# A new order, engine choice and buffer choice for the 822 tasks of a sparse attention and maxout kernel

## The chip, the cores and the metric

The kernel runs on one NeuronCore of a Trainium2 chip. Its five engines run their own instruction queues in order: TensorE (PE in the profile) for matmuls and transposes, VectorE (DVE), ScalarE (ACT), GpSimd (POOL) and SyncE (SP), which issues DMAs. Data moves between HBM and the on-chip memory SBUF by DMA; PE writes its results to eight banks of PSUM, which DVE and ACT read. The metric is device time in microseconds (us) of one execution, the median of several runs.

## The reference

Four batches, eight heads, 768 positions of 64 values. Each position attends to its neighbours closer than 16 and to 24 block summaries (the maximum of k, the mean of v over blocks of 32). A two-branch maxout layer follows, in which the two hidden products are compared element by element.

```python
k_sum = k.reshape(B, H, nb, block, D).max(axis=3)
v_sum = v.reshape(B, H, nb, block, D).mean(axis=3)
scores_l = np.where(mask_l, scale * q @ k.T, -1e9)
scores_s = scale * einsum('bhsd,bhnd->bhsn', q, k_sum) + log(block)
a = softmax(concatenate([scores_l, scores_s], axis=-1))
x = heads_side_by_side(a @ concatenate([v, v_sum], axis=2))   # 3072 x 512
out = np.maximum(x @ w1, x @ w2) @ w_out                       # 512 -> 1024 -> 512
```

Inputs and output are float32; the matmuls run in bf16.

## The kernel before, in words

The kernel writes the work down as a list of tasks (`Plan.op`): each has a label, the engines that could do it, the buffers it reads and writes, and a function that issues its instructions. `Plan.run` then sends the tasks out in an order given by hand (`CFG["order"]`, numbers of tasks), each on the engine that a letter names (`CFG["engines"]`: T for PE, D for DVE, A for ACT, P for POOL, S for SP) and into the buffer of a ring that a character names (`CFG["slots"]`). Each engine therefore runs its tasks in the order in which they stand in the list, and waits for what it reads, and for the last readers of a buffer that it writes again. Nothing else sets the order: there is no planner at run time.

A label such as `x 021` has the batch (0), the group of 256 positions (2) and the first of two pairs of heads (1 stands for its pair); `wd 10` has the half of the hidden units (1) and of the input rows (0). What the labels mean, in the order of the data:

- `load k03`, `load q03`, `load v03` (L334, L343): one pair of heads of one batch is loaded from HBM, 384 KB, by a DMA from SP into a ring of 13 buffers `land`. A load waits until the former content of its buffer has been read. Loads of k, and most of q, read runs of 1536 bytes (two to a partition), loads of v and of six q (w in the label) runs of 256.
- `cast` (L254 on POOL, L256 elsewhere): to bf16. POOL does it in two or three instructions.
- `turn k`, `turn q` (L463): transposes on PE into PSUM, followed by `place` (L256), the copy into SBUF. For six pairs of heads of batches 2 and 3, k and q, a transposing DMA from SP (`dturn`, L467) does this.
- `max k` (L487), `wrap`, `tails`, `sums k` (L256): the block maxima of k and the copies that put local keys and summaries side by side in `kx`.
- `odd v`, `sums`, `esums`, `all sums` (L387, L424, L254, L256): v in the second alignment, and the block sums of v, made on PE with `amean` and copied into `vx`.
- `hides` (L518, batch 0) or `mask` (L549): the positions that do not count. `scores` (L529), `exp` (L541, on ACT), `values` (L569), `inv` and `x` (L587, L590, on DVE): the attention. x goes into `xt` in transposed form, for batch 0 by PE (`turn x`, L605, and a copy `xt`), for the others by a transposing DMA (`dxt`, L596).
- `load w`, `load wo` (L620, L651), `wd` (L630, the difference of the two weights), `w1b`, `turn w1`, `w1t`, `wo`: the weights, once. `w1o` (L662) is w1 times w_out, so that out = x @ w1o + relu(x @ (w2 - w1)) @ w_out.
- `hidden` (L678), `relu` (L690 on ACT, L692 on DVE), `outx` and `outg0`, `outg1` (L715), `copy out` (L256), `store` (L729, and L731 where an output block wraps around the end of the batch): the layer after attention, in 12 groups of 256 positions, each with four hidden tasks of 8 matmuls (in batch 0 in two halves) and two outputs of 12 matmuls. The second half of the very last group (`320`) is cut into 256, 128 and 128 columns.
- `filler` (L750): 30 matmuls on zeros, whose result nobody reads.

The order of the tasks in `Plan.op` calls is fixed by the code; the three strings of CFG only say when, where and into which buffer.

Of the kernel before, what the change touches and what calls it, by code (L numbers as in the profile page):

```python
# [24 lines left out]
PPPDPDPPPDDPDPPPTTTTTTTTTTTTTTTTTTTTTTTTTTTTTTSSSPDDDTDDDSSSPADATDDPSSSADAATAPPSSSADDATAAASSPDTASSPATASSPDTDSSDDTASPSD  # L25
SPSAPTPTDDADDDDTPTDDAAADATATDDPPPDPTDTADPAADTTATTDDTDTTATTDDTATTATTDDTDTTATTDDTATTATTDDTATTATTDDTDSSSPSSSPSSSDSSSDDDAD
DPTDDAPDADAPATPTDDAAPDATATDDDDDADTPTDDDDPDPTATADAAAATADTTDDSTADTTDDSTADTTDDSTADTTDDSTADTTDDSTADTTDDSSSSASSSASSSPSSSDDD
PDDPPTDAPDDDPPDATPTDDDADDDTPTADDDPDPSASDDPPAASDSADAPATADTTDDSTADTTDDSTADTTDDSTADTTDDSTADTTDDSTADTTDDSSSSPSSSASSSPSSSDP
ADDAAPTDPPDAPPPADSPSADPPDDSDSDDAAPPSDSADADDASPSDDAAPTADTTDDSTADTTDDSTADTTDDSTADTTDDSTADTTDDSTADTTDDSTTATTATTATTATTATTA
TTATTDTTTDATTTDSTTDTTATTATTDTTTDSTTTDATTATTATTDTTATTTAATTTAATATDTATATTTAATTTASTATDTATATTTDSTTTAATATATDTATTTASTTTASTATD  # L30
TDTDTTTDATTTDSTDTATATDTTTDATTTDSTATATATATTTAATTTDSTATDTDTDTTTAATTTDSTDTDTDTDTTTAATTTDSTATATATDTTTASTTTAATTTAATTTDA
""".split())
CFG["order"] = list(map(int, """
# [778 lines left out]
```

## Time and profile before

| | |
|---|---|
| runs | 166.24, 166.53 and 202.32 us; median 166.53 |
| profiled execution | 168.04 us, of which 166.1 are the span from first to last instruction |
| busy in the span | PE 153.8, DVE 108.7, ACT 97.0, POOL 66.3 us |
| DMA | 36.48 MB, 25.18 MB read from HBM and 6.29 MB written to it |
| granted TensorE clock | 1.0 throughout |

The profile's page has, after the busy times, the span in 40 slices (each digit the busy share in tenths), the DMA queues, the chain of work that ended last, and groups of instructions by line, engine and shape with their busy time, the mean duration in ns, and the idle time of the engine just before them with what ended it. A timeline row has the start in us, the time in us, engine and line, output and inputs, and in brackets the idle time before it and its releaser. PE's busy time includes the fillers.

### The profile page before, as it was taken

What the parts mean: (1) busy time and instruction counts of PE and PEld (TensorE: products, weight loads), DVE (VectorE), ACT (ScalarE), POOL (GpSimd) and SP (SyncE); (2) the same over time, 40 slices, a digit from 0 to 9 for tenths busy, and PEclk for the clock granted to TensorE, in tenths of its full rate; (3) what the DMA queues carried; (4) which work ended last, traced back from release to release, by engine and by line L of the source; (5) the groups of instructions that cost most, each with busy time, mean ns of one, the idle gap of its engine ahead of it and who ended that gap; (6) DMA issues with size and microseconds to landing.
All of it is one profiled execution on the core that took longest, in us unless ns stands there. A gap on an engine that the chain in (4) does not pass through costs nothing.

```text
span 166.1 us, 4394 instructions
## 1 busy us (share of the span) xinstructions
PE 153.8 (93%) x1760; PEld 100.1 (60%) x1782; DVE 108.7 (65%) x210; ACT 97.0 (58%) x140; POOL 66.3 (40%) x136
## 2 busy tenths in 40 slices
PE   4696769999999999999999999999997999999995
PEld 1244456998655554577578555676545657756763
DVE  3188698739847699799598575759865777161310
ACT  3158999756897579648965596544666721010511
POOL 5876547952458076323699230010919000000000
PEclk9999999999999999999999999999999999999999
DMA  5999999999999999399899998799998515930354
GB/s 158 286 301 295 234 318 390 385 381 382 307 255 220 310 361 182 88 203 175 151 231 190 258 276 133 151 216 229 210 168 210 171 46 156 180 123 4 113 206 129
DMA packets 67988, 36.48 MB, mean 220 GB/s; under 512 B 54912, under 2 KB 61952, under 8 KB 67968
## 3 DMA queue, kind: packets, MB, share of 16 engines
q1 hardware_dynamic: 65648, 33.04, 81.6%
q10 hardware_dynamic: 2320, 3.16, 6.7%
q8 instruction: 14, 0.23, 0.6%
q14 instruction: 6, 0.05, 0.1%
HBM read 25.18 MB, written 6.29 MB: 189 GB/s over the span
## 4 chain that ended last, share of the span: by engine, by line
PE 69%; DMA 10%; DVE 5%; SPq 5%; ACT 4%; issue 2%; POOL 2%; POOLq 0%; DVEq 0%; ACTq 0%
PE banks L715 31%; PE banks L678 20%; DMA land<-in_k_dram 7%; SPq L334 5%; PE banks L662 4%; PE banks L569 4%; PE banks L463 3%; DMA kt<-kqb 3%; PE banks L529 3%; POOL vx L254 2%; DVE xs L590 1%; DVE vx L256 1%; ACT kqb L256 1%; PE banks L639 1%; PE banks L750 1%
## 5 line engine op out<-in xcount | busy, mean ns | idle before, releaser
L678 PE MATMUL banks<-xt,wd 128*128 128x256 bf16 x384 | 45.4, 273 | 0.9 <-DMA xt<-xs 0.9
L715 PE MATMUL banks<-wo,g 128*128 128x512 bf16 (+2 forms) x198 | 45.1, 362 | 0.9 <-issue 0.6
L678 PEld LDWEIGHTS <-wd 128*128 128x128 bf16 x384 | 37.0, 98 | 7.4 <-issue 1.1
L715 PEld LDWEIGHTS <-g 128*128 128x128 bf16 x208 | 19.1, 98 | 18.8
L541 ACT ACTIVATE pb<-banks 128x1024 bf16<-128x1024 f32 x24 | 23.6, 1021 | 7.8 <-PE banks L529 7.6
L690 ACT ACTIVATE g<-banks 128x512 bf16<-128x512 f32 x28 | 16.1, 598 | 17.3 <-PE banks L678 17.1
L715 PE MATMUL banks<-w1o,xt 128*128 128x512 bf16 (+2 forms) x96 | 23.8, 362 | 0.9 <-issue 0.3
L254 POOL CAST kqb<-land 128x256 bf16<-128x256 f32 (+1 forms) x35 | 16.3, 501 | 17.8 <-DMA land<-in_k_dram 7.7
L692 DVE TENSOR_SCALAR g<-banks 128x512 bf16<-128x512 f32 x20 | 13.4, 685 | 14.0 <-PE banks L678 13.3
L254 POOL COPY vx<-sums 32x396 bf16<-32x396 bf16 x26 | 15.7, 629 | 6.9 <-DVE sums L256 6.3
L256 ACT COPY o<-banks 128x512 f32<-128x512 f32 (+2 forms) x13 | 7.0, 544 | 18.0 <-PE banks L715 10.8
L590 DVE TENSOR_TENSOR xs<-banks,inv 128x512 bf16<-128x512 f32 x24 | 16.4, 690 | 0.6
L487 DVE TENSOR_REDUCE ks<-kx 128x24 bf16<-128x768 bf16 x16 | 14.9, 939 | 2.0 <-ACT kx L256 1.8
L715 PEld LDWEIGHTS <-xt 128*128 128x128 bf16 x104 | 9.6, 98 | 8.9 <-issue 0.4
L549 DVE TENSOR_TENSOR pb<-pb,mask 128x1024 bf16<-128x1024 bf16 x18 | 13.0, 750 | 2.2 <-ACT pb L541 2.1
L256 DVE COPY o<-banks 128x512 f32<-128x512 f32 (+1 forms) x13 | 8.3, 652 | 8.7 <-PE banks L715 8.7
L463 PE MATMUL banks<-ident,kqb 128*128 128x128 f32 x60 | 10.1, 279 | 2.7 <-DVE kqb L256 1.3
L569 PEld LDWEIGHTS <-pb 128*64 128x64 bf16 x384 | 7.7, 110 | 6.4 <-issue 4.0
L750 PE MATMUL banks<-zeros,identity 128*128 128x512 bf16 x27 | 9.4, 466 | 2.3 <-DVE identity L237 2.2
L463 PEld LDWEIGHTS banks<-ident,kqb 128*128 128x128 f32 x60 | 7.1, 140 | 6.2 <-ACT kqb L256 1.8
L569 PE MATMUL banks<-vx,pb 128*64 128x65 bf16 x384 | 9.6, 196 | 1.4 <-DVE vx L256 1.0
L256 ACT CAST kqb<-land 128x768 bf16<-128x768 f32 x10 | 9.5, 953 | 2.3 <-DMA land<-in_k_dram 2.1
(78 smaller groups left out, 179.2 us busy)
## 6 DMA issues: line engine op xcount, KB each, us to landing
land<-in_k_dram SPq DMA_DIRECT2D x16, 384.0 KB, 5.9
land<-in_q_dram SPq DMA_DIRECT2D x16, 384.0 KB, 6.3
land<-in_v_dram SPq DMA_DIRECT2D x16, 384.0 KB, 6.3
land<-in_moe_w_dram SPq DMA_DIRECT2D x8, 512.0 KB, 9.4
out_dram<-o ACTq DMA_DIRECT2D x10, 256.0 KB, 2.9
out_dram<-o SPq DMA_DIRECT2D x9, 256.0 KB, 3.3
land<-in_moe_w_out_dram SPq DMA_DIRECT2D x4, 512.0 KB, 10.1
out_dram<-o SPq DMA_DIRECT2D x3, 224.0 KB, 3.0
```

Source lines behind the costliest of these rows:

```text
L254: nc.gpsimd.tensor_copy(out=o[:, n * z:n * z + n], in_=i[:, n * z:n * z + n])
L256: {"D": nc.vector.tensor_copy, "A": nc.scalar.copy, "P": nc.gpsimd.tensor_copy}[e](out=o, in_=i)
L463: nc.tensor.transpose(out=bank(ps)[:, 128 * j:128 * j + 128], in_=src.ap[:].bitcast(F32)[:, 128 * j:128 * j + 128], identity=ident32[:])
L487: op("D", lambda e: nc.vector.tensor_reduce(out=ks.ap[:, 0:nb], in_=free(kt(), 128, [256, NM], [192, 2], [32, 2], [1, 32]), axis=AX.X, op= ...
L541: op("A", lambda e: nc.scalar.activation(out=spread(pb.ap[:, 0, 0:1], [1, 1024]), in_=spread(bank_tile[:, ps.ap, 0:1], [1, 1024]), func=AC ...
L549: on(e).tensor_tensor(out=o.rearrange("p n (u c) -> p n u c", u=2), in0=o.rearrange("p n (u c) -> p n u c", u=2), in1=in1, op=ALU.mult)
L569: nc.tensor.matmul(out=av(n)[64 * par:64 * par + 64, u, a, :], lhsT=pb.ap[r, at, 64 * par:64 * par + 64], rhs=rhs, start=start, stop=stop)
L590: op("D", lambda e: nc.vector.tensor_tensor(out=x.ap[:].rearrange("p n u a d -> p n (u a) d"), in0=spread(bank_tile[:, ps.ap, 0:1], [512, ...
L678: nc.tensor.matmul(out=bank(ps)[:, 256 * s:256 * s + 256], lhsT=wd[n // 2][:, c, 256 * (n % 2) + 128 * s:256 * (n % 2) + 128 * s + 128], r ...
L690: nc.scalar.activation(out=o, in_=bank(ps), func=ACT.Relu)
L692: nc.vector.tensor_scalar_max(out=o, in0=bank(ps), scalar1=0.0)
L715: nc.tensor.matmul(out=bank(ps, c1 - c0), lhsT=a, rhs=w, start=(i == j == 0), stop=(i == 2 and j == 3))
```

## The change

All three strings are replaced; the functions that make the tasks stay as they are, so both kernels have the same 822 tasks with the same dependencies. The order, the engine letters and the buffer characters were searched anew against a replay in which shared ports and queues are granted strictly in order of time. The diff, cut to its first and last lines:

```diff
 CFG["engines"] = "".join("""
-PPPDPDPPPDDPDPPPTTTTTTTTTTTTTTTTTTTTTTTTTTTTTTSSSPDDDTDDDSSSPADATDDPSSSADAATAPPSSSADDATAAASSPDTASSPATASSPDTDSSDDTASPSD
...
+PDPPDPDDPDPPDDPPTTTTTTTTTTTTTTTTTTTTTTTTTTTTTTSSSDDDDTADADSSSPDAPTDAPSSSAAAPTADASSSADDPTDDDSSPATASSPATASSDATDSSDATDSDSD
...
 CFG["order"] = list(map(int, """
-26 33 36 24 23 39 43 38 19 17 25 13 8 1 10 79 46 57 152 2 14 153 156 9 11 6 12 132 133 136 122 123 126 137 158 3 138
...
-814 815 816 37 29 35 20 28 45
+46 44 8 10 41 21 24 38 20 79 36 122 43 25 26 32 42 123 40 17 6 5 9 11 3 13 152 2 14 12 7 16 198 126 127 59 60 64 28 65
...
+802 803 793 804 30 805 806
 """.split()))
 CFG["slots"] = "".join("""
-21307350100567735176041164504713:20254416874209;71<0001211340787130912213221010031111222322013302361011622101070220060
...
+32131016101270510013030211110705722362618:40019;01<0061215541436000821000202020332111303323112210200000104042246161121
...
 """.split())
```

Read out, with the numbers turned into labels:

| | before | after |
|---|---|---|
| tasks on PE, DVE, ACT, POOL, SP | 291, 207, 153, 69, 102 | 291, 223, 150, 51, 107 |
| cast of k or q on DVE, ACT, POOL | 9, 10, 13 | 12, 11, 9 |
| cast of v on DVE, ACT, POOL | 4, 5, 7 | 7, 5, 4 |
| all sums on DVE, ACT, POOL | 11, 8, 13 | 15, 10, 7 |
| wd on DVE, POOL | 1, 3 | 2, 2 |
| wo (cast) on DVE, ACT, POOL | 1, 1, 2 | 3, 1, 0 |
| relu on ACT, DVE | 28, 20 | 25, 23 |
| stores from ACT, SP | 14, 12 | 9, 17 |

SP's queue begins, before: k03, k00, k01, q00, v01, q01, k02, v02, q02, q03, v00, v03, then w100, w200, w201, w101, w110, w210, k11, k13, w211, w111. After: k00, k03, v01, k01, v02, q00, q01, v00, k02, q03, q02, v03, then w100, w200, w101, w201, w111, w210, w110, w211, k12, wo1, k10, k13, k11.

PE's queue begins, before, with 11 fillers and turn k03, k01, k00, q00; further fillers stand up to just ahead of the first hidden task (hidden 0200, with turn x 021 ahead of it), and six at the very end. After, 12 fillers, turn k00, and 17 more fillers between hides, sums and turns, all ahead of the first scores; the first hidden task is 0210, with turn w1 00, turn x 021 and turn x 022 ahead of it; one filler stands at the end.

The last attention of batch 3, before: scores 300, 301, 302, later 320, 322, 321. After: scores 321, 320, 322, later 302, 301, 300. PE's queue ends, before: outputs 321, then 320 in its three pieces. After: hidden 310, the pieces of 320 between outputs 300 and 301, then outputs 311, 310, 311 (its last part) and 321.

More of the change, by code (lines that the diff above doesn't have):

```diff
@@ L29 @@
-ADDAAPTDPPDAPPPADSPSADPPDDSDSDDAAPPSDSADADDASPSDDAAPTADTTDDSTADTTDDSTADTTDDSTADTTDDSTADTTDDSTADTTDDSTTATTATTATTATTATTA
-TTATTDTTTDATTTDSTTDTTATTATTDTTTDSTTTDATTATTATTDTTATTTAATTTAATATDTATATTTAATTTASTATDTATATTTDSTTTAATATATDTATTTASTTTASTATD
-TDTDTTTDATTTDSTDTATATDTTTDATTTDSTATATATATTTAATTTDSTATDTDTDTTTAATTTDSTDTDTDTDTTTAATTTDSTATATATDTTTASTTTAATTTAATTTDA
+PDPPDPDDPDPPDDPPTTTTTTTTTTTTTTTTTTTTTTTTTTTTTTSSSDDDDTADASSSPDAPTDAPSSSAAAPTADASSSADDPTDDDSSPATASSPATASSDATDSSDATDSDSD
+SDSAATPTDDAAADPTDTDDADDADTPTDDAADDPTDTDDPPPDTTATTDDTDTTATTDDTDTTATTDDTATTATTDDTDTTATTDDTATTATTDDTDSSSDSSSASSSDSSSDADDP
@@ new lines @@
+ADTDADDDDDDDDTDTADPPADDTATDDPAPAPTDTADDADDATDTDDAAPATADTTDDSTADTTDDSTADTTDDSTADTTDDSTADTTDDSTADTTDDSSSSPSSSPSSSDSSSADD
+AADAATAAAPPDPPDATATADPDADPTATDDPAPDDSASDDDDDASPSDDAPATADTTDDSTADTTDDSTADTTDDSTADTTDDSTADTTDDSTADTTDDSSSSDSSSPSSSASSSDD
+DPDAPDTAAAPPDADAPSASDDAPADSDSDDPADASASADDADDSPSDDDDATADTTDDSTADTTDDSTADTTDDSTADTTDDSTADTTDDSTADTTDDSTTATTDTTATTATTATTA
+TTATTATTTASTTTASTTATTDTTDTTDTTTDSTTTASTTATTATTDTTATTTDSTTTASTATDTDTDTTTAATTTDSTDTATDTDTTTASTTTDSTDTATDTATTTASTTTAATATD
+TATDTTTDSTTTASTDTATATATTTAATTTDATDTDTDTATTTDSTTTDSTDTDTATATTTDATTTASTATATATDTTTAATTTDSTDTATDTATTTAATTTDSTTTDATTTDA
@@ L68 @@
+432033426227224010096;;37794:5<2032350140212325171220124251000221334340121420400423040025232115020813:9468<02371231203
+2102300041032212204412143000222212204036121000342218;10:47<32651100151212042013330025213164402562420212133444016361142
+0223263042323746551271406270115616361037541202326627020077407421302100510021021162733030550676234531054645102655451076
 """.split())
```

6 lines of the change are left out of this document (removed), and 52 rows, old and new, of the table turn.

## The prediction

> **What bounds the kernel now.** I read the page's first two parts, then the busy time in three stretches cut at the first matmul of the hidden layer (29.27 us) and at the last matmul of an output (163.1 us), then who made PE wait in the middle stretch.
>
> ```profile
> span 166.1 us, 4394 instructions
> PE 153.8 (93%) x1760; PEld 100.1 (60%) x1782; DVE 108.7 (65%) x210; ACT 97.0 (58%) x140; POOL 66.3 (40%) x136
> DMA  5999999999999999399899998799998515930354
> ```
>
> ```profile
> core 0: us, PE busy (x) PEld busy (x) DVE busy (x) ACT busy (x) POOL busy (x), PEclk, DMA share, GB/s
> 0.00:29.27 29.27, 21.59 (x298) 12.87 (x301) 19.56 (x46) 19.48 (x29) 19.33 (x53) 1.00 1.01 284
> 29.27:163.10 133.83, 130.95 (x1461) 86.84 (x1478) 89.14 (x165) 77.29 (x111) 46.99 (x84) 1.00 0.88 209
> 163.10:166.10 3.00, 1.23 (x5) 0.39 (x4) 0.00 (x0) 0.27 (x1) 0.00 (x0) 1.00 0.28 87
> ```
>
> ```profile
> PE banks L715 <- issue: 1.0, 6, 0.2
> PE banks L678 <- DMA xt<-xs: 0.9, 1, 0.9
> ```
>
> The span is 29.27 of lead-in, 130.95 of PE work, 2.88 of PE idle (133.83 - 130.95) and 3.0 of tail. Of the idle time one wait stands out, 0.9 us for a transposing DMA; the rest is small. So a new order of the same PE tasks has at most 2.9 us to win in the middle; what else it wins must come from the lead-in or the tail. The profiled execution took 168.04 us, 1.94 more than its span; the median of the runs is 166.53, 0.43 over the span. I sum the span and add 0.43.
>
> **The lead-in.** No PE task is added or removed, so the first term is when the hidden layer may start. Two things set it: the weights (wd 00, the difference of the first two weight blocks) and the last x of batch 0.
>
> ```profile
> 7.00 5.71 DMA land<-in_k_dram
> 18.50 0.96 POOL L254 CAST vx<-land 128x384 bf16<-128x384 f32 x2 [1.96 <-DMA land<-in_v_dram]
> 24.05 2.78 POOL L630 TENSOR_TENSOR wd<-land,land 128x256 bf16<-128x256 f32 x4 [2.09 <-DMA land<-in_moe_w_dram]
> 29.27 1.47 PE L678 MATMUL banks<-xt,wd 128*128 128x256 bf16 x12
> ```
>
> The seventh load (k02) lands at 12.71 and the eleventh (v00) is taken up at 18.50: (18.50 - 12.71) / 4 = 1.45 us a load, with the DMA engines full. The change reorders the first twelve loads (v01 and v02 before q00; v00 eighth instead of eleventh; q02 eleventh instead of ninth), but w100 and w200 stay the thirteenth and fourteenth. So wd 00 can start at about 24 us as before and, on POOL again, ends at 24.05 + 2.78 = 26.8. That is a floor for the first hidden matmul: at most 29.27 - 26.8 = 2.4 us can be won. The floor itself can rise:
>
> ```profile
> L630 POOL TENSOR_TENSOR wd<-land,land x12: 721/726/1264, 24.0 to 33.5; 128x256 bf16<-128x256 f32 x12
> ```
>
> Most of these take 0.72 us, the slowest 1.26; with four slow ones wd 00 ends at 24.05 + 4 x 1.26 = 29.1. The Trainium skill (GPSIMD Engine Reference, section 1, Specifications) says that POOL's SBUF interfaces are shared with VectorE, and this change makes VectorE busier just there. The spread of the row agrees with it; by that rule the upper end would be the likelier one. The median being 0.726 while DVE was 90% busy, I take 27.5.
>
> The other condition is DVE's chain.
>
> ```profile
> 7.67 0.59 DVE L256 CAST kqb<-land 128x768 bf16<-128x768 f32 x1 [1.02 <-DMA land<-in_k_dram]
> 10.56 0.96 POOL L254 CAST vx<-land 128x384 bf16<-128x384 f32 x2 [0.48 <-DMA land<-in_v_dram]
> 20.00:30.00 10.00, 8.42 (x207) 6.19 (x208) 9.07 (x22) 9.21 (x14) 6.92 (x12) 1.00 1.01 343
> 30.38 0.69 DVE L590 TENSOR_TENSOR xs<-banks,inv 128x512 bf16<-128x512 f32 x1
> L487 DVE TENSOR_REDUCE ks<-kx 128x24 bf16<-128x768 bf16 x16 | 14.9, 939 | 2.0 <-ACT kx L256 1.8
> L256 DVE CAST kqb<-land 128x768 bf16<-128x768 f32 x9 | 5.4, 605 | 2.1 <-DMA land<-in_q_dram 1.1 <-DMA land<-in_k_dram 1.0
> L256 DVE COPY qx<-banks 128x768 bf16<-128x768 bf16 x8 | 4.3, 548 | 1.2 <-PE banks L463 1.1
> L590 DVE TENSOR_TENSOR xs<-banks,inv 128x512 bf16<-128x512 f32 x24 | 16.4, 690 | 0.6
> ```
>
> Before, PE enters the hidden layer with x 022 still to come (it starts at 30.38). After, PE's queue has the turns of x 021 and x 022, and the turn of one weight block, ahead of the first hidden task. In DVE's new queue, place k03 stands behind esums 01, and that needs v01. The third load lands by 7.65 (first row); POOL casts k03 first and writes the ones of amean, to 8.1, then v01 in 1.0; sums, esums and the turn of k03 take some 1.3 more: 10.4. From place k03 to the end of x 022 stand 37 DVE tasks: three maxima (0.94), three casts of k and q (0.60), six placings (0.55), five x (0.69), and twenty of 0.2 to 0.6, 7.1 together: 2.8 + 1.8 + 3.3 + 3.5 + 7.1 = 18.5 us. Neighbouring DVE instructions overlap by 6% (all durations sum to 116, the page has 108.7 busy), so 17.4; DVE was idle for 0.9 of the ten us from 20 to 30, and I add the same. x 022 ends at 10.4 + 17.4 + 0.9 = 28.7, and with turn and wait the first hidden task starts at **29.0**, 0.3 earlier than before. Bounds: 27.0 (wd at its floor, DVE's tasks shorter by a tenth) and 31 (a slow wd, and DVE idle for a fifth of the time).
>
> Behind it PE has 130.95, less the turns now ahead (0.22 for the x, 0.44 for the weights): **130.3**.
>
> **The middle.** Eighteen compute tasks leave POOL (69 to 51): casts of v and q, copies of sums, wd 10 and both halves of wo. Sixteen go to DVE (207 to 223). With the mean durations of their groups POOL loses 24 us, DVE gains 9 and ACT 2; five stores go from ACT's queue to SP's. On PE's path none of this costs anything as long as DVE keeps up: 108.7 + 9 = 118 us in 163. Its cover is thin where its tasks crowd: in the thirty PE microseconds around the last part of batch 2 DVE would stand at 27 instead of 22. A store issue costs SP about 0.5 us, and the dxt and dturn transposes queue behind it, five times 0.5 = 2.5 in all, spread over 100 us of PE work that hides it; of 0 to 2.5 I take 0.
>
> ```profile
> GB/s 158 286 301 295 234 318 390 385 381 382 307 255 220 310 361 182 88 203 175 151 231 190 258 276 133 151 216 229 210 168 210 171 46 156 180 123 4 113 206 129
> 27.69 4.01 POOL L630 TENSOR_TENSOR wd<-land,land 128x256 bf16<-128x256 f32 x5 [0.86 <-DMA land<-in_moe_w_dram]
> ```
>
> The eight w loads are now the 13th to the 20th, with k11 and k13 no longer among them. A w load (524 KB) takes 1.35 us at the 390 GB/s of the best slice and 1.8 at the pace from wd 00 to wd 01 (two loads from 24.05 to 27.69), so the 20th lands between 32 and 35, and k11, the 25th, between 38 and 42. PE reaches its turn 13 us of work behind the first hidden task, at 42. This just holds; a wait of 1 us is possible.
>
> The 0.9 us wait for xt<-xs goes away where it stood, since the last attention now lies earlier in PE's order; I let a new one of the same size take its place. Idle: **2.9**, between 1.5 and 8.5 (the upper end is the second rival's).
>
> **The tail.** Before, the last output is cut (256, 128, 128 columns), so the last copy and store are small. After, this cut group comes first, and the last PE task is outg1 321, uncut, with a copy of 512 columns and two stores (112 and 16 rows) behind it, all on ACT.
>
> ```profile
> 160.47 0.59 ACT L256 COPY o<-banks 128x512 f32<-128x512 f32 x1 [2.85 <-PE banks L715]
> 162.47 0.61 PE L715 MATMUL banks<-wo,g 128*128 128x128 bf16 x8
> 163.21 0.27 ACT L256 COPY o<-banks 128x128 f32<-128x128 f32 x1 [1.06 <-PE banks L715]
> 163.50 0.34 ACTq L729 DMA_DIRECT2D out_dram<-o  x1
> out_dram<-o ACTq DMA_DIRECT2D x10, 256.0 KB, 2.9
> out_dram<-o ACTq DMA_DIRECT2D x1, 224.0 KB, 3.4
> out_dram<-o ACTq DMA_DIRECT2D x2, 64.0 KB, 1.7
> ```
>
> Before: matmuls end at 163.08, issue at 163.50, landing 1.7 later at 165.2, and 0.9 to the end of the span: 3.0. After: copy 0.6, then a landing of 2.9 (the median of the large ones) and the same 0.9: 4.4. If the two issues follow one another (0.4) and take 3.4, it is 5.3; with the ends of all waits as short as for the small store, 3.5. I take **4.3**: 1.3 us dearer.
>
> **Sum.** 29.0 + 130.3 + 2.9 + 4.3 = 166.5, or +0.4 on the span; 166.53 + 0.4 = **166.9 us**. I call this no change: 2% (3.3 us) is about what a measurement of this kernel can tell from none.
>
> **Rivals.**
>
> 1. *Everything fits, faster.* First hidden at 27.0, idle 1.5, tail 4.0: 27.0 + 130.3 + 1.5 + 4.0 = 162.8 on the span, **163.2**. For it: the weights' floor is 26.8 and v00, taken up at 18.50 before, is three places further ahead. Against: DVE's 18.5 us. Chance 0.17; it is over 2% faster in half of these at most.
>
> 2. *The last transposes come late, slower.* The place is the last batch's scores 321.
>
> ```profile
> 118.44 0.58 SPq L334 DMA_DIRECT2D land<-in_q_dram  x1
> 124.17 0.95 POOL L254 CAST kqb<-land 128x384 bf16<-128x384 f32 x2 [3.39 <-DMA out_dram<-o]
> 120.51 5.85 SPq L467 DMA_TRANSPOSE kt<-kqb  x3
> 129.22 0.67 PE L529 MATMUL banks<-kt,kx 64*128 64x64 bf16 x36
> 32.52 3.49 PE banks L678 x32
> 44.86 1.73 PE banks L662 x8
> ```
>
> Before, q33 is loaded last (issued 118.44), cast at 124.17, turned by DMA (issued by 126.4) and used from 129.22 on. At 0.87 for a hidden task (8 of 109 ns) and 0.86 for four wide matmuls, 34.4 us of PE work stood behind the first scores of this last half (129.22 + 34.4 = 163.6, against 163.1). After, 40.3 us stand behind them: they have to be ready 6 us earlier, at about 162 - 40.3 = 121.8. The queue has less ahead of q33 by then (one load of 1.45, four transposes, of which three took 5.85 to issue), 6 to 9 us, so it just comes out. If the DMAs bring q33 when they did before, PE waits 6 us: 166.5 + 5.6 = 172.1, **172.5**. It decides from a landing of q33 after 118. Chance 0.15.
>
> 3. *PE's clock falls in the lead-in.* The filler matmuls now all stand ahead of the scores of heads 0 to 3; before, four stood between the values and the first hidden tasks.
>
> ```profile
> 2.21 4.47 PE L750 MATMUL banks<-zeros,identity 128*128 128x512 bf16 x11 [2.21 <-DVE identity L237]
> 10.30 0.59 PE L750 MATMUL banks<-zeros,identity 128*128 128x512 bf16 x2
> ```
>
> Eleven fillers took 4.47 us, 0.4 each, at the start; two took 0.59 later, the second starting 0.21 after the first. So the early ones ran at half pace. Should the 8 to 9 us of PE work of the last ten ahead of the hidden layer (8.42 in the row of 20 to 30 us) run so in part, 2 to 4 us are added, **169.9**. Against it: DVE feeds PE steadily there. The Trainium skill (TensorE: Matmul & The Clock Gate, Part 1) has the clock fall back only after an idle window of about 3.4 us; by that rule this rival costs nothing, and the pace of the first row agrees with its warm-up. Chance 0.06.
>
> **Chances.** Forecast 0.62 (its own range 165.2 to 168.7), rival 1 0.17, rival 2 0.15, rival 3 0.06. Faster by over 2% (under 163.2): half of rival 1 and a little of the forecast, 0.10. Slower by over 2% (over 169.9): rival 2 and half of rival 3, 0.18. The same: 0.72. The range, 163.7 to 170.6, leaves out part of rival 1 and the full price of rival 2.
>
> **What would show it.** The first hidden matmul between 28.3 and 29.7 us, PE busy time behind it within 1 us of 130 and idle 2 to 4, a tail over 4 us that ends in a 224 KB store from ACT, DVE near 117 and POOL near 45 busy. Wrong would be: a hidden layer from 27 on with idle under 2 (rival 1), a PE wait of several us ahead of the last batch's scores released by kt<-kqb or the copies behind it (rival 2), or matmuls of batch 0 at twice their spacing (rival 3).

## The result and the profile after

The changed kernel takes 170.76 us (median of four runs, 170.48 to 171.3); the kernel before, run beside it, 166.76. The ratio is 1.0254 with a 95% interval of 1.021 to 1.0299: slower, by about 4 us. The prediction said 166.9. One of the four runs of the kernel before, of 202.32 us, fell into a slower state of the chip and is left out of the ratio.

The profiled execution took 171.3 us, 169.5 of them span. First the page's two parts, then the busy time in the same three stretches as before, cut at the first matmul of the hidden layer and at the last one of an output:

```profile
span 169.5 us, 4376 instructions
PE 154.6 (91%) x1762; PEld 100.8 (59%) x1782; DVE 113.9 (67%) x226; ACT 99.7 (59%) x142; POOL 44.3 (26%) x98
DMA  4999999999999995259999993799995156410642
```

```profile
core 0: us, PE busy (x) PEld busy (x) DVE busy (x) ACT busy (x) POOL busy (x), PEclk, DMA share, GB/s
0.00:28.54 28.54, 23.49 (x317) 14.39 (x319) 21.14 (x52) 19.59 (x28) 17.67 (x50) 1.00 1.03 308
28.54:165.42 136.88, 130.96 (x1449) 86.41 (x1465) 92.74 (x175) 79.55 (x114) 26.58 (x48) 1.00 0.83 200
165.42:169.50 4.08, 0.20 (x1) 0.00 (x0) 0.00 (x0) 0.59 (x1) 0.00 (x0) 1.00 0.21 64
```

Against the rows of before: the lead-in is 0.73 shorter (28.54 against 29.27), the middle 3.05 longer (136.88 against 133.83), the tail 1.08 longer (4.08 against 3.00). Together 3.4, which is 169.5 - 166.1. PE's busy time in the middle is the same to 0.01, so the 3.05 us are PE's idle time: 5.92 where it was 2.88. (Both traces lack some twenty matmul records, 1760 and 1762 against 1782 weight loads, which shows as small "issue" gaps in both.)

A word on the labels: in `x 122` and `scores 302` the second figure is the first of two pairs of heads (0 or 2) and the third the group of 256 positions; the section on the kernel has these two the wrong way round. Hidden tasks, outputs and stores have the group second.

Where PE waits is read from its timeline; the bracket holds the idle time ahead of a row and what ended it. These are all gaps of 0.2 us and more behind the first hidden matmul:

```profile
67.52 0.57 PE L569 MATMUL banks<-vx,pb 128*64 128x65 bf16 x24 [0.43 <-DVE pb L549]
68.72 0.45 PE L569 MATMUL banks<-vx,pb 128*64 128x65 bf16 x16 [0.63 <-DVE xs L590]
79.33 2.56 PE L678 MATMUL banks<-xt,wd 128*128 128x256 bf16 x22 [1.54 <-DMA xt<-xs]
115.77 1.03 PE L678 MATMUL banks<-xt,wd 128*128 128x256 bf16 x8 [0.27 <-DVE g L692]
129.07 0.69 PE L529 MATMUL banks<-kt,kx 64*128 64x64 bf16 x36 [0.99 <-DMA kt<-kqb]
146.24 0.28 PE L715 MATMUL banks<-w1o,xt 128*128 128x128 bf16 x2 [0.31 <-DMA xt<-xs]
```

They sum to 4.2 us, so smaller gaps make up 1.75 of the 5.92. Three places carry the sum. The values of batch 1 (67.5 and 68.7) wait for a mask and for an x, both on DVE. The hidden task at 79.33 waits for the transposing DMA of x 122. The scores at 129.07 wait for the transposed q 30. The kernel before has two gaps of this size, 1.15 us together, and 1.73 in smaller ones:

```profile
125.48 2.56 PE L678 MATMUL banks<-xt,wd 128*128 128x256 bf16 x22 [0.93 <-DMA xt<-xs]
128.26 1.02 PE L715 MATMUL banks<-w1o,xt 128*128 128x512 bf16 x3 [0.22 <-ACT g L690]
```

What lay ahead of x 122 in SP's queue is seen in SP's own rows, in the order of issue:

```profile
68.70 5.65 SPq L596 DMA_TRANSPOSE xt<-xs  x4
74.40 0.57 SPq L729 DMA_DIRECT2D out_dram<-o  x1
75.07 1.22 SPq L596 DMA_TRANSPOSE xt<-xs  x1
```

Four transposes, the store of output 010, then the transpose of x 122: the queueing that the prediction had costed at nothing. But the store is not what PE waited for. It put the issue off by 0.67 us, to 75.07; the transpose then took 4.2 us to land, where 2.4 is usual (last section). With 2.4 it would have landed at 77.5, before PE stopped at 77.79 (79.33 - 1.54).

### The profile page after: what moved, and what is told of

Its sections match the earlier page's. It is cut to its first block, busy times and chain, and to the rows that moved or that the text cites. A ratio compares the mean times of both kernels' runs of the same rounds, so it can differ in the third digit from the quotient of the medians.

```text
span 169.5 us, 4376 instructions
## 1 busy us (share of the span) xinstructions
PE 154.6 (91%) x1762; PEld 100.8 (59%) x1782; DVE 113.9 (67%) x226; ACT 99.7 (59%) x142; POOL 44.3 (26%) x98
## 4 chain that ended last, share of the span: by engine, by line
PE 55%; DVE 18%; DMA 15%; SPq 5%; issue 3%; ACT 1%; POOL 0%; DVEq 0%; POOLq 0%
PE banks L715 24%; PE banks L678 16%; DMA xt<-xs 7%; DVE vx L256 6%; DMA kt<-kqb 4%; PE banks L662 4%; DMA land<-in_v_dram 4%; PE banks L569 3%; SPq L334 3%; DVE kx L256 2%; PE banks L463 2%; PE banks L529 2%; DVE xs L590 2%; DVE ks L487 2%; DVE pb L549 2%
## 5 line engine op out<-in xcount | busy, mean ns | idle before, releaser
L690 ACT ACTIVATE g<-banks 128x512 bf16<-128x512 f32 x25 | 14.6, 597 | 24.2 <-PE banks L678 16.3
L692 DVE TENSOR_SCALAR g<-banks 128x512 bf16<-128x512 f32 x23 | 15.5, 686 | 13.8 <-PE banks L678 13.7
L715 PE MATMUL banks<-w1o,xt 128*128 128x512 bf16 (+2 forms) x91 | 23.2, 361 | 1.3 <-issue 0.3
L254 POOL CAST kqb<-land 128x256 bf16<-128x256 f32 (+1 forms) x24 | 12.1, 536 | 33.9 <-PE banks L463 9.4
L256 DVE COPY o<-banks 128x512 f32<-128x512 f32 (+2 forms) x13 | 7.7, 603 | 13.7 <-PE banks L715 13.7
L256 ACT COPY o<-banks 128x512 f32<-128x512 f32 x13 | 7.4, 589 | 12.7 <-PE banks L715 12.7
L549 DVE TENSOR_TENSOR pb<-pb,mask 128x1024 bf16<-128x1024 bf16 x18 | 12.2, 694 | 2.4 <-ACT pb L541 2.3
L256 ACT COPY vx<-vx 32x1320 bf16<-32x1320 bf16 (+4 forms) x10 | 9.9, 995 | 4.7 <-POOL vx L254 3.3
L750 PE MATMUL banks<-zeros,identity 128*128 128x512 bf16 x29 | 10.1, 483 | 1.8 <-DVE sums L267 1.6
L529 PEld LDWEIGHTS <-kx 64*128 64x128 bf16 x416 | 7.0, 94 | 5.2 <-issue 3.5
```

What stands on the lines that cost most here:

```text
L254: nc.gpsimd.tensor_copy(out=o[:, n * z:n * z + n], in_=i[:, n * z:n * z + n])
L256: {"D": nc.vector.tensor_copy, "A": nc.scalar.copy, "P": nc.gpsimd.tensor_copy}[e](out=o, in_=i)
L549: on(e).tensor_tensor(out=o.rearrange("p n (u c) -> p n u c", u=2), in0=o.rearrange("p n (u c) -> p n u c", u=2), in1=in1, op=ALU.mult)
L690: nc.scalar.activation(out=o, in_=bank(ps), func=ACT.Relu)
L692: nc.vector.tensor_scalar_max(out=o, in0=bank(ps), scalar1=0.0)
L715: nc.tensor.matmul(out=bank(ps, c1 - c0), lhsT=a, rhs=w, start=(i == j == 0), stop=(i == 2 and j == 3))
```

## Experiments

Each edit moves entries of the order string or changes letters of the engine string, with all tasks and dependencies kept; the diffs name the tasks. Times are medians of five rounds, the ratio is to the kernel before on the same chip (166.6 to 167.0 us). A median moves by about 1 us within its interval, so effects below that are read from the traces and not from the times.

**The visible waits, one by one.** First a store out of a transpose's way.

```diff
 SP queue
-dxt 102, store 010, dxt 122, load q22
+dxt 102, dxt 122, store 010, load q22
```

> The changed kernel with one edit: the store of output 010 is put behind the transposing DMA of x 122 in SP's queue. Theory A (a store ahead of a transpose costs its issue time): the transpose is issued at about 74.4 us instead of 75.07 and PE's wait of 1.54 us at 79.33 shrinks by 0.7 us; if the late landing (4.2 us where 2.4 is usual) came from the store's own traffic, the wait goes altogether: 170.8 less 0.7 to 1.5, so 169.3 to 170.1. Rival B (the landing is held up by something else that stands at a fixed time, such as the fetch of code at 76.6 to 77.9 us): the transpose still lands at about 79.3 and the time stays at 170.8 within 0.3.

Measured: 170.97 us, 1.0244 (1.0188 to 1.0299), no change. PE's gaps of 0.2 us and more from 64 to 130 us in this run:

```profile
66.83 0.58 PE L569 MATMUL banks<-vx,pb 128*64 128x65 bf16 x24 [0.43 <-DVE pb L549]
68.34 0.45 PE L569 MATMUL banks<-vx,pb 128*64 128x65 bf16 x16 [0.93 <-DVE xs L590]
83.96 1.90 PE L715 MATMUL banks<-wo,g 128*128 128x512 bf16 x8 [0.69 <-ACT g L690]
113.81 0.81 PE L678 MATMUL banks<-xt,wd 128*128 128x256 bf16 x6 [0.85 <-DMA xt<-xs]
128.19 0.69 PE L529 MATMUL banks<-kt,kx 64*128 64x64 bf16 x36 [0.20 <-DMA kt<-kqb]
```

The wait of 1.54 us at 79 is gone, as theory A said, and the time stays, as rival B said, though not for its reason: new waits stand at 83.96 (relu 100 on ACT) and 113.81 (x 222). What PE gained it waited for again.

Next the tail, undone in the changed kernel and put into the kernel before:

```diff
 PE queue of the changed kernel
-outg 320 (256), outg 320 (128), ..., outg 311, outg 310, outg 311, outx outg0 outg1 321
+..., outg 311, outg 310, outg 311, outx outg0 outg1 321, outg 320 (256), outg 320 (128)
```

> The changed kernel with its last outputs in another order: the pieces of 256 and 128 columns of output 320 come behind the uncut output 321, and the store of the last piece goes from SP. Theory A (the tail is 1.1 us dearer because it ends in an uncut copy and a 224 KB store): the stretch behind the last output matmul falls from 4.08 us to about 3.1, the time by 1.0 to 169.8. Rival: the store of 321 lands just as late since the tail is bound by the bytes still to be written; then the time falls by at most 0.4, to 170.4.

> The kernel before, with only its tail changed: output 321 uncut comes last, behind the pieces of output 320, and its store goes from ACT, as in the changed kernel. Theory A (the uncut end costs 1.1 us of the loss): 166.7 plus 0.7 to 1.1, so 167.4 to 167.8, and the stretch behind the last output matmul grows from 3.0 to about 4.1 us. Rival (the last landing is set by bytes in flight, not by the cut): 166.7 within 0.3.

Measured: 170.87 us, 1.0255 (1.0194 to 1.0316), for the tail undone, and 169.11 us, 1.015 (1.011 to 1.019), for the tail in the kernel before. The last stretches of the two, and the one new wait of the second:

```profile
165.50:168.90 3.40, 0.21 (x1) 0.00 (x0) 0.30 (x2) 0.00 (x0) 0.00 (x0) 1.00 0.43 135
```

```profile
162.79:166.90 4.11, 1.46 (x6) 0.48 (x5) 0.00 (x0) 0.58 (x1) 0.00 (x0) 1.00 0.21 64
```

```profile
157.36 0.60 PE L715 MATMUL banks<-w1o,xt 128*128 128x256 bf16 x4 [0.78 <-DVE o L256]
```

Undone, the stretch falls from 4.08 to 3.40; put in, it rises from 3.00 to 4.11. So the uncut end costs 0.7 to 1.1 us of trace time. The edit in the kernel before cost 2.5 us in time, more than either theory: 1.1 is the tail and 0.78 a wait for a bank that the new place brought with it; the rest isn't placed. (Its trace is only 0.8 us longer than that of before, since the wait of 0.93 us at 125 is missing in it.) The edit in the changed kernel did not show in the median.

Then DVE's crowd. These are three stretches of four microseconds around the values of batch 1 in the changed kernel:

```profile
60.00:64.00 4.00, 3.95 (x80) 2.25 (x76) 3.79 (x11) 3.93 (x6) 0.69 (x2) 1.00 1.16 288
64.00:68.00 4.00, 3.51 (x47) 1.81 (x45) 3.85 (x9) 3.70 (x6) 1.76 (x3) 1.00 0.51 110
68.00:72.00 4.00, 3.32 (x45) 1.64 (x42) 3.51 (x9) 2.53 (x3) 0.00 (x0) 1.00 0.26 50
```

The columns are PE, PEld, DVE, ACT, POOL, clock, DMA share. DVE and ACT are full, POOL stands, PE begins to lose time and the DMA engines run dry (0.51 and 0.26), since the transposes wait for DVE's x.

```diff
 engines
-D  cast v10, odd v122h, all sums 110, all sums 130, all sums 131
+P  cast v10, odd v122h, all sums 110, all sums 130, all sums 131
```

> The changed kernel with five tasks of batch 1 (cast of v 10, half a difference of v 12, the sums of heads 11, 13 and 13) on POOL instead of DVE; they take 2.07 us on DVE between 57 and 67 us, where DVE is busy without a break and POOL for 2.5 of 10 us. Theory A (DVE's crowd makes PE wait): PE's waits at 67.5 and 68.7 (0.43 and 0.63 us) go, and the transposes of batch 1's x start up to 2 us earlier, so that the wait at 79.33 shrinks too: 170.8 less 1.0 to 2.5, so 168.3 to 169.8. Rival (the stretch is bound by the late loads of v 10 and v 11, or POOL at 1.0 us for one such task is late itself): no gain, 170.5 to 171.5.

Measured: 170.67 us, 1.02 (1.0146 to 1.0254). The same stretches:

```profile
60.00:64.00 4.00, 4.00 (x67) 2.16 (x66) 3.62 (x8) 3.95 (x5) 3.84 (x7) 1.00 1.10 269
64.00:68.00 4.00, 3.51 (x61) 1.95 (x59) 3.90 (x7) 3.71 (x6) 3.53 (x5) 1.00 0.59 145
68.00:72.00 4.00, 4.00 (x73) 2.37 (x72) 3.20 (x9) 2.00 (x3) 0.00 (x0) 1.00 0.49 98
```

PE gains 0.73 us in these twelve (11.51 busy against 10.78). Of this, 0.57 is the two waits: the one for the mask (0.43) is gone, the one for x is 0.49 instead of 0.63; the rest is gaps so small that missing records make them too. The wait for the mask stands, with 0.43 to 0.45 us, in eleven traces of the changed order without this edit and in none of the four with it, so DVE's crowd does cost there. The intervals of the times overlap, so the time can't say how much of it reaches the end.

Then the wait for q 30, by stores put behind what they stood ahead of:

```diff
 SP queue
-dturn k30, store 001, load q33, dturn k31, dturn q32, store 111, load q30, dturn q33, store 201, store 110, dturn q31, dturn q30
+dturn k30, load q33, dturn k31, store 001, dturn q32, load q30, dturn q33, store 111, dturn q31, dturn q30, store 201, store 110
```

> The changed kernel with four stores (outputs 001, 111, 201, 110) moved behind loads and transposes of batch 3 in SP's queue, so that the load of q 30 is issued 0.6 to 1.1 us earlier and two stores no longer stand between the transposes of q 33 and q 31. Theory A (stores ahead of transposes cost their issue time): the transpose of q 30 lands at 127.5 to 128.3 instead of 128.93, PE's wait of 0.99 us at 129.07 falls to 0.4 or less, and the time by 0.6 to 1.0, to 169.8 to 170.2. Rival (the load of q 30 is bound by the DMA engines' bytes, not by its place): landing and wait stay, 170.8 within 0.3.

Measured: 170.89 us, 1.0242 (1.0192 to 1.0292). The wait at 129 falls under 0.2 us, but that is no proof of the edit: it is missing too in the run with the tail undone and in the one with relu 100 ahead of k 32 (below), where these entries stand as in the changed kernel. Where PE comes later to these scores, q 30 is there. Two other waits stand earlier:

```profile
85.05 1.90 PE L715 MATMUL banks<-wo,g 128*128 128x512 bf16 x8 [0.85 <-ACT g L690]
114.85 0.81 PE L678 MATMUL banks<-xt,wd 128*128 128x256 bf16 x6 [0.85 <-DMA xt<-xs]
```

The edit lies behind 112 us, yet the wait of 1.54 us at 79 isn't in this trace either and the one for relu 100 is. Here store 010 still stands ahead of x 122, which was issued at 75.19 and landed 2.4 us later. So which of the waits between 75 and 86 us shows differs from one execution to the next, and the first run's edit is not shown to be what removed the one at 79; in each of the traces so far one of the two is paid.

And the wait that the first run had uncovered, with store 010 moved as there:

```diff
 ACT queue
-cast k32, relu 100
+relu 100, cast k32
```

> The changed kernel with store 010 behind the transpose of x 122, as before, and besides the cast of k 32 put behind relu 100 in ACT's queue. In the run with the store alone PE's wait for x 122 had gone and a new one of 0.69 to 0.85 us for relu 100 stood at 84 us, and relu 100 stood on ACT behind that cast, which waits for the load of k 32. Theory A (the wait moved to the next thing that was late by as much): relu 100 comes 0.8 us earlier, the 0.7 us wait goes, and the excess between 70 and 90 us falls from 2.0 to 0.6, the time by about 1 to 169.8. Rival (time won before 100 us is waited for again at 113 us, for x 222, and at 128 us, for q 30): 170.8 within 0.4, with the trace's stretch from 70 to 90 shorter all the same.

Measured: 170.97 us, 1.025 (1.0208 to 1.0292). Between 70 and 90 us no gap of 0.2 us is left; a new one of 0.44 stands at 98 and one of 0.73 for x 222 at 115. The rival was right: the place has no wait left, and the time is the same.

**Is SP's issuing the price?**

```diff
 engines
-S  store 010, 011, 000, 101, 120, 001, 111, 201, 110, 021, 020, 200, 220, 221
+A  store 010, 011, 000, 101, 120, 001, 111, 201, 110, 021, 020, 200, 220, 221
```

> The changed kernel with its 14 stores ahead of the last batch's outputs issued from ACT instead of SP, places in the order unchanged. Theory C (SP's queue itself is the bound from about 100 to 128 us, where it issues without a break, and again from 69 to 82 us): 14 x 0.55 = 7.7 us of issuing leave SP, six of them in the 28 us from 100 to 128, PE's waits for transposed x and k in 70 to 130 us shrink together by 1.5 to 3, and the time falls to 168 to 169.5. Rival (SP is late only because x and loads come late; ACT, which now issues the stores at 0.35 us each between exps and copies, gets later itself): 170.3 to 171.5.

Measured: 173.94 us, 1.0393 (1.0335 to 1.045). Slower than the changed kernel, by 2.3 us (the difference of the two ratios, times 166.8 us), so theory C fell: SP's half microsecond for a store is not what is lost. That ACT has less room for the stores than SP is argued and not shown by a trace. The Trainium skill (DMA: Bandwidth & Descriptors, section "Issuing engines are not separate DMA queues") says that issuing from another engine saves only the time on the sequencer that starts the transfer; this run, which is slower, shows no other saving either.

**Loads and transposes in SP's queue.** Three edits move the loads of k 30 and k 31 (and store 120) backwards:

```diff
 SP queue, changed kernel
 dxt 221, store 120, load k30, load k31, dxt 202, dturn k33, dxt 222, load q31
 SP queue, first edit
+dxt 221, dxt 202, store 120, load k30, load k31, dxt 222, dturn k33, load q31
 SP queue, second edit
+dxt 221, dxt 202, store 120, load k30, load k31, dturn k33, dxt 222, load q31
 SP queue, third edit
+dxt 221, dxt 202, dturn k33, dxt 222, store 120, load k30, load k31, load q31
```

> The changed kernel with the store of output 120 and the loads of k 30 and k 31 put behind the transpose of x 202 in SP's queue, and the transpose of k 33 behind that of x 222. Theory A (what stands ahead of a transpose in SP's queue delays it): the transposes of x 202 and 222 land about 2 us earlier, at 110 to 112, PE's wait of about 1 us in front of the hidden tasks of x 222 (113 to 115 us in the last four runs) goes, and if nothing else takes its place the time falls by 1.0, to 169.8. Rival (the saved time is waited for again further on, at the last batch's scores of q 30, whose load now starts later): 170.6 to 171.2.

> The changed kernel with only store 120 and the loads of k 30 and k 31 behind the transpose of x 202 in SP's queue; the transpose of k 33 keeps its place ahead of x 222. In the run that moved both, DVE stood at the placing of k 33 from the transpose that had been put back, and relu 201 behind it. Theory A (that transpose was what made the run slower, and the loads ahead of x 202 do cost): 169.5 to 170.2, without the wait of 1 us for x 222 at 113. Rival (the loads are needed where they were: k 30 and k 31 come late): 171 to 172.

> The changed kernel with store 120 and the loads of k 30 and k 31 behind the transpose of x 222 in SP's queue, so that no load stands ahead of the transposes of x 202, k 33 and x 222; those three keep their order. Theory F (a transposing DMA lands only when the loads issued ahead of it have landed, some 1.5 us for each; five loads moved ahead cost 5 us, and in the two runs with k 30 and k 31 behind x 202 they stood directly ahead of x 222): x 222 lands by 110 us instead of 113.8, the waits of 0.8 to 1.6 us at 113 to 116 go, the loads land within 1 us of where they did, and the time falls by 0.5 to 1.2, to 169.7 to 170.4. Rival (the waits come back at 128 us, for the later k 30 and q 30): 170.9 within 0.4, with the trace's 110 to 120 shorter.

Measured: 172.46 us, 1.0327 (1.0279 to 1.0374); 172.05, 1.0307 (1.0258 to 1.0356); 173.43, 1.0363 (1.0311 to 1.0415). The third is clearly slower than the changed kernel; the intervals of the first two overlap with its (1.021 to 1.0299), so that they lose is likely and no more. None wins. In the first, DVE stood 4.38 us at the placing of k 33, whose transpose had been put back, relu 201 stood behind it, and PE waited for that:

```profile
115.08 0.83 DVE L256 COPY kx<-kt 128x768 bf16<-128x768 bf16 x1 [4.38 <-DMA kt<-kqb]
```

```profile
117.55 1.03 PE L678 MATMUL banks<-xt,wd 128*128 128x256 bf16 x8 [1.54 <-DVE g L692]
```

The third has no load ahead of the three transposes, and PE does not wait for x 222, as it did in the traces above (0.7 to 0.9 us at 113 to 115). In its place, on PE:

```profile
119.85 1.03 PE L678 MATMUL banks<-xt,wd 128*128 128x256 bf16 x8 [1.30 <-DVE o L256]
127.95 0.79 PE L529 MATMUL banks<-kt,kx 64*128 64x64 bf16 x44 [1.65 <-DMA kt<-kqb]
132.36 0.69 PE L529 MATMUL banks<-kt,kx 64*128 64x64 bf16 x36 [1.41 <-DMA kt<-kqb]
```

DVE stood 3.05 us at the cast of k 31 with a copy that frees a bank behind it, and k 30 and q 30 came later for the last scores. Theory F held in direction at its place and not in size: x 222 landed at 113.0 instead of 113.8, and not by 110; and the two loads that were put back landed 4.8 and 5.0 us later, and not 1.

The opposite, loads forwards:

```diff
 SP queue, last five loads
+load v33, load k30, load k31, load q31, load q33, load q30, dxt 220
 SP queue, middle loads
+load q23, load q22, load k32, load v30, load v31, dxt 120
```

> The changed kernel with the last five loads (k 30, k 31, q 31, q 33, q 30) moved up in SP's queue, right behind the load of v 33, so that they are issued before the transposes of batch 2's last x instead of behind and between them. Their buffers are free by 76 us. Theory E (the loads stand in SP's queue behind transposes that wait for x, so the DMA engines run at 0.53 of their time from 100 to 108 us and are full from 108 to 128, where these loads and the transposes of x 202, x 222, k and q collide): the DMA share in 100 to 108 rises, the wait for x 222 at 113 and the one for q 30 at 128 go, and the excess of 110 to 130 falls from 2.8 to 3.2 to about 1; the time falls by 1.5 to 2.5, to 168.3 to 169.3. Rival (five loads, 7 us of DMA time, delay the transposes of x 220 to x 221, which are waited for at once): 171 or more.

> The changed kernel with the loads of q 22, k 32 and v 30 moved up in SP's queue behind the load of q 23, and that of v 31 ahead of the transpose of x 120, so that they run while SP waits for x 120. Theory E (the DMA engines stand at 0.26 to 0.56 of their time from 64 to 76 us, since these loads queue behind transposes that wait for x): the wait of 1.5 us for x 122 at 79 and that of 0.7 for relu 100 at 84 both go, since the transposes of 75 to 84 us have fewer loads between them and k 32 is there early; the time falls by 1 to 1.5, to 169.3 to 169.8. Rival (the time won is waited for again at 113 and 128 us): 170.8 within 0.4.

> The loads of both runs moved up, nothing else. Theory E: the two gains add, 2.5 to 4 us, so 166.8 to 168.3. Rival (one place takes up what the other gives): not better than the better one of the two.

> Both groups of loads moved up, the pieces of output 320 last and five tasks of batch 1 on POOL. Theory E with the two shown terms (tail 0.7, DVE's crowd 0.5 to 1.0): 165 to 167, no slower than before. Rival (the waits move on again): 168.5 to 169.8, as without the loads.

Measured: 176.37 us, 1.0565 (1.0528 to 1.0602), for the last five loads; 174.19, 1.0384 (1.0328 to 1.044), for the middle ones; 178.34, 1.0685 (1.0633 to 1.0737), for both; 177.95, 1.0628 (1.0566 to 1.0689), with tail and POOL besides. Theory E fell: all four are clearly slower than the changed kernel, the middle loads by 2.2 us and the last five by 5.2 (differences of the ratios). The run with the last five shows why, in SP's rows and PE's:

```profile
97.37 1.86 SPq L334 DMA_DIRECT2D land<-in_k_dram  x2
99.27 6.61 SPq L334 DMA_DIRECT2D land<-in_q_dram  x3
105.99 6.09 SPq L596 DMA_TRANSPOSE xt<-xs  x4
```

```profile
110.74 1.89 PE L678 MATMUL banks<-xt,wd 128*128 128x256 bf16 x8 [5.00 <-DMA xt<-xs]
```

SP needed 6.61 us to issue three loads, and the transpose of x 220, issued at 99.91 in the changed kernel, went out at 105.99. The half-empty DMA engines from 100 to 108 us were no spare room: in that time single transposes come one by one for work that PE takes at once, and the five loads put in there made PE wait 5.00 us. Part of the loss is the clock: after that wait the granted clock stood at 0.50 from 110.65 to 114.06 us. The page of the Trainium skill just named (section "Queues, rings and completion order") has each DMA engine take descriptors in the order of its ring; in this trace the five loads and the transpose behind them landed in the order of issue, the last load at 109.60 and the transpose at 110.11 us, which agrees. Why the middle loads cost time is not worked out.

The same rule tried on the kernel before, where a load stood directly ahead of a transpose that PE waited for:

```diff
 SP queue of the kernel before
-dxt 202, load q33, dxt 222, dturn k32, dturn q32
+dxt 202, dxt 222, load q33, dturn k32, dturn q32
```

> The kernel before, with the load of q 33 put behind the transpose of x 222 in SP's queue instead of directly ahead of it; nothing else. Theory F: x 222, which took 6.4 us to land behind that load, lands in 2.5 to 4 us, PE's loss of 1.1 us at 125 us goes; q 33 lands 1 us later at most, and 0.3 us of the gain may go to the last batch's scores: 165.6 to 166.2 where before has 166.7. Rival (x 222 was late for other reasons, or q 33 is the tighter of the two): 166.5 to 168.

Measured: 168.09 us, 1.0055 (1.0024 to 1.0087): slower by 0.9 us, where a gain was expected. The DMA issues around it, first before and then in this run (kind, count, median us from issue to landing):

```profile
xt<-xs SPq DMA_TRANSPOSE x1, 6.4
```

```profile
xt<-xs SPq DMA_TRANSPOSE x2, 2.5
```

```profile
120.47 7.40 SPq L467 DMA_TRANSPOSE kt<-kqb  x3
```

```profile
126.23 1.50 ACT L256 COPY kx<-kt 128x768 bf16<-128x768 bf16 x1 [3.18 <-DMA kt<-kqb]
```

```profile
128.53 1.02 PE L715 MATMUL banks<-w1o,xt 128*128 128x512 bf16 x3 [1.61 <-ACT g L690]
```

x 222 landed in 2.5 us instead of 6.4, and the wait for it went, as theory F had it. But now the transposes of k and q stood behind the load; three of them took 7.40 us to issue where they had taken 5.85. ACT stood 3.18 us at the placing of k 32, the relus of the same hidden layer stood behind it, and PE waited 1.61 us for those instead of 0.93 for x. In both orders what stands behind the load pays for it.

**All repairs together, and the engines alone.**

```diff
 first set: tail, POOL, SP queue
+dxt 122, store 010; stores 001, 111, 201, 110 as for q 30; dxt 202, store 120, load k30, load k31, dxt 222, dturn k33
 second set: tail, POOL, SP and ACT queues
+dxt 122, store 010; relu 100, cast k32; dxt 202, store 120, load k30, load k31, dturn k33, dxt 222
 engines alone, on the kernel before
+all 822 letters of the changed kernel
```

> All edits at once: store 010 behind the transpose of x 122, the tail's pieces last, five tasks of batch 1 on POOL, stores of batch 3 behind its loads and transposes, and the loads of k 30 and k 31 behind the transpose of x 202. Theory A (each place costs its own wait, and a single edit shows little because the next place takes it up): the repairs add up to 0.7 for the tail, 1.1 for 60 to 70 us, 1.2 for 70 to 90 and 1.0 for 110 to 120: 170.8 less 4, about 167. Rival (the time from 120 us on is set by the last batch's loads and transposes, at fixed times): only the tail's 0.7 is won, 170.0.

> The changed kernel with the pieces of 320 last, five tasks of batch 1 on POOL, store 010 behind the transpose of x 122, the cast of k 32 behind relu 100, and the loads of k 30 and k 31 behind the transpose of x 202. Theory A (waits add up): 0.7 + 1.0 + 1.2 + 0.8 less than 170.8, so 167.1. Rival (a chain of SP's queue and loads at the pace of the DMAs sets the time from 110 us on): only the tail is won, 170.0.

> The kernel before, its order and buffers kept, with the engines of the changed kernel for all copies and stores (191 tasks differ). Theory D (DVE's 5 to 9 us more work, crowded between 57 and 76 us, is what makes the changed kernel slower): slower than before by 2 to 4, 168.7 to 171. Rival (the order is what costs: where stores and loads stand in SP's queue, and the tail): within 1 us of before, 166 to 167.7. The engines were not meant for this order, so a loss above 4 us would say nothing for either.

Measured: the first set of repairs 170.27 us, 1.0223 (1.018 to 1.0267), the second 169.82, 1.0161 (1.0123 to 1.0199). The second set's interval lies below the changed kernel's (1.021 to 1.0299), so it does win, 1 to 1.5 us of the 3.7 that the terms added up to. The rivals, which gave 170.0, were nearer in both. The engines of the changed kernel on the order of before give 208.88 us, 1.2502 (1.2444 to 1.256); by what was written ahead of it a loss of that size says nothing for either theory, and it is not used.

## Why the prediction was wrong

**The sum, term by term.** Lead-in: 29.0 was forecast, 28.54 measured, 0.5 less. PE's work behind it: 130.3 forecast, 130.96 measured, 0.7 more. PE's idle time: 2.9 forecast, 5.92 measured, 3.0 more. Tail: 4.3 forecast, 4.08 measured, 0.2 less. From the span to the median of the runs: 0.43 forecast, 170.76 - 169.5 = 1.26 measured, 0.8 more, because the profiled execution of before took 1.5 us more than the median (168.04 against 166.53) and that of the changed kernel 0.5 more (171.3 against 170.76). Together, unrounded, this is the 3.8 us between 166.93 and 170.76.

**The step that failed** is the idle term, "2.9, between 1.5 and 8.5". It carried over the idle time of before, with its one wait of 0.9 us in a new place, and took two costs at nothing. Measured were 5.92. Of the 3.0 us more, 1.9 are waits for transposing DMAs (1.54 for x 122, 0.99 for q 30 and 0.31 at 146 us, where before had 0.93), and 1.3 are waits for DVE (0.43, 0.63 and 0.27, where before had none); a wait of 0.22 for ACT is gone.

One cost at nothing is the sentence on SP's queue: "five times 0.5 = 2.5 in all, spread over 100 us of PE work that hides it; of 0 to 2.5 I take 0". PE's work did not hide the late transposes. But the runs do not show that the five stores made them late: with store 010 behind x 122, with four stores behind what they stood ahead of and with fourteen stores on ACT the time did not fall, and the wait for x 122 came from its late landing and not from its place. What did delay a transpose by microseconds is a load ahead of it (6.4 against 2.5 us for x 222); the cast or placing that waits for the transpose then holds up relus and copies on DVE and ACT. The other cost is DVE: "On PE's path none of this costs anything as long as DVE keeps up". The cover was thin one batch earlier than the prediction put it, not in the last part of batch 2 but in the values of batch 1, at 57 to 69 us, where 1.06 us of PE's waits stand behind DVE, and 0.57 of them go when five tasks leave it.

**What held.** The lead-in's chain: DVE's place k 03 started at 10.1 us where 10.4 was worked out, and x 022 ended at 28.2 where it was 28.7. (The half microsecond is one execution's: with the clock at 1.00 the lead-in took 28.0 to 28.9 us in nine traces of this order, and 29.2 to 29.3 in three of the order before.) The weights' floor did not rise but fell: the last of the four subtractions of wd 00 ended at 22.07 + 3.02 = 25.1 and not 26.8. The slow subtractions that the upper bound allowed for did not come, though DVE was busier in the lead-in (21.1 us against 19.6); the eight that are left on POOL have a median of 0.729 us and none above 0.854:

```profile
L630 POOL TENSOR_TENSOR wd<-land,land x8: 722/729/854, 22.1 to 27.8; 128x256 bf16<-128x256 f32 x8
```

The tail was right in mechanism and within 0.2 us in size: copy of 0.59, two issues from ACT, then the landing.

```profile
165.44 0.59 ACT L256 COPY o<-banks 128x512 f32<-128x512 f32 x1 [2.87 <-PE banks L715]
166.06 0.34 ACTq L729 DMA_DIRECT2D out_dram<-o  x1
166.44 0.44 ACTq L731 DMA_DIRECT2D out_dram<-o  x1
```

DVE is at 113.9 (near 117 was forecast), POOL at 44.3 (45).

**The rivals.** Rival 2 named the right kind of wait, transposes that come late, and the wrong place: no wait of 0.2 us stands at scores 321, which were to decide it; 0.99 us stands at scores 302 for q 30, and 1.54 us much earlier, at x 122. Its price of 6 us in one place came as 2.84 us of waits in three. Rival 1 fell: the first hidden matmul came at 28.54 and not 27.0, and the idle time was 5.92 and not 1.5; only its tail of 4.0 came. Rival 3 did not happen in the changed kernel's own trace, whose granted clock is 1.00 in all three stretches, but its mechanism is real: in six of fourteen traces of edited kernels with the same lead-in the clock fell there (last section). It does not explain the loss. A fall of the length seen would take 0.01 off the mean clock of a run, and the four runs of the changed kernel have 0.995 to 1.0.

**What is shown and what stays open.** Shown: 0.7 to 1.1 us of trace time for the tail, from both sides; 0.57 us of PE's waits for DVE's crowd; that the single waits seen in one trace are not the terms of a sum. In five runs the wait that the edit aimed at was gone (at 79, 84, 129 and 113 us, and at 125 us in the kernel before) and the time the same or longer, though the waits at 79 and 129 were missing in traces without the edit too. Shown by the opposite moves is also that the loads in SP's queue from some 65 to 130 us have little slack in either direction: moved right back they cost 1.8 us by the ratios, moved forward 2.2 and 5.2. Open is which property of the new order makes the remaining loss, 2.7 us with the second set of edits (ratio 1.0161); no single edit and neither set recovers it. The kernel before is the fastest version measured.

## What to carry to other kernels

Where one queue carries loads, stores and the transposes that the compute engines wait for, cost every load ahead of a transpose as a delay of that transpose, then follow the delay through the in-order queue of the engine that waits for it; don't spread the sum over the whole stretch and call it hidden. A new order with the same tasks and the same busy times can be slower only by its waits and its two ends, so the idle time is the term that needs a range of its own from the queues, not the value of before carried over. And one visible wait in one trace is not a price: remove it, look where the next stands, and look whether the wait is there in a second execution without the edit, before counting a gain.

## What the runs showed of the hardware that was not expected

**A fetch of instructions beside a transposing DMA.** The page's DMA part counts 14 packets of 16 KB of kind "instruction" on their own queue in each run. In the changed kernel one of them, from 77.0 to 78.0 us, falls into the flight of x 122, between 75 and 79.3 us (queue, kind, packets, MB, share; then the transposes issued there):

```profile
q8 instruction: 1, 0.02, 1.5%
...
xt<-xs SPq DMA_TRANSPOSE x1, 4.2
```

In the run with store 010 moved, no such packet falls between 73.6 and 76.1 us, and the same transpose takes:

```profile
xt<-xs SPq DMA_TRANSPOSE x1, 2.4
```

There the store behind it meets the packet and takes 4.2 us instead of 2.4. In the run for q 30, with the queue as in the changed kernel, the packet came only at 77.4 us, 2.2 after the issue, and x 122 landed in 2.4 as well. Over eighteen traces (those of the stores on ACT and of the engines alone are left aside), transposes of x with no transfer from SP or ACT other than transposes of x ahead of them in flight landed in 2.40 to 3.53 us without such a packet (86 of them, median 2.47) and in 2.41 to 4.35 with one (41). Six of the 41 took 3.9 or more; in these six, and in no other, the packet began 1.8 to 2.1 us after the issue. That the fetch is the cause is argued from this agreement, not tried by itself. It would explain why the wait at 79 us comes and goes between executions whose code is the same up to there.

**The clock in the lead-in.** The same lead-in, in the run for q 30:

```profile
0.00:29.24 29.24, 23.95 (x318) 15.34 (x318) 20.37 (x52) 20.14 (x29) 17.63 (x50) 0.94 1.03 308
```

The figure 0.94 is the granted clock, which is 1.00 in the changed kernel's own trace. It stood at half from 25.7 to 29.1 us. In six traces it fell so for 3.41 us, first between 18 and 27 us, and these lead-ins took 28.7 to 31.5 us. In the 3.41 us ahead of the first fall PE had idled 1.1 to 1.9 us, never more than 1.5 in one piece, so the idle window of about 3.4 us by which the prediction ruled this out is not a condition here. Why it falls in some executions of the same code and not in others was not tried.
